# Threshold attention with hash-routed experts: expert tiles of 122 slots in place of 128, and expert 0's blocks turned elsewhere

## The chip, the cores and the metric

The kernel runs on one core of a Trainium2 chip. The metric is the device time in microseconds (us) of one execution; lower is better. The engines are TensorE (PE; its weight loads are listed apart as PEld), VectorE (DVE), ScalarE (ACT), GpSimd (POOL) and SyncE (SP), and sixteen DMA engines carry the transfers that SP and POOL issue.

## What is computed

Attention with a threshold, over 8 batches of 8 heads with 576 rows of 64, is followed by a layer of 8 experts. A token's expert is a hash of its id, with no learned gate, and each token goes to exactly one expert. All is float32.

```python
# attention: batch 8, heads 8, seq 576, head_dim 64
scores = scale * np.matmul(q, k.transpose(0, 1, 3, 2))
thresh = np.max(scores, axis=-1, keepdims=True) - tau
scores = np.where(scores >= thresh, scores, -1000000000.0)
attn = np.exp(scores - np.max(scores, axis=-1, keepdims=True))
attn = attn / (np.sum(attn, axis=-1, keepdims=True) + 1e-09)
x = np.matmul(attn, v)            # -> (B*S, H*D) = (4608, 512)
# experts: N 4608, D 512, E 8, F 1024
expert_idx = token_ids * np.int64(2654435761) % np.int64(E)
for e in range(E):
    mask = expert_idx == e
    h = np.maximum(x[mask] @ w1[e], 0.0)
    out[mask] = h @ w2[e]
```

The inputs are drawn with a fixed seed. The token ids of that seed give the eight experts 598, 596, 571, 565, 599, 533, 570 and 576 tokens.

## The kernel before

**Attention.** The 64 pairs of batch and head are taken two heads at a time: 32 "pairs" p of five steps s, so 160 steps n = 5p + s, and six more steps drain the pipeline (L508; `LAST` is 160). A step takes 128 rows of each of its two heads; step s = 0 takes the last 64 rows of both together. The order of instructions on each engine is the order in which this loop writes them (`manual_schedule`, L500), and the engines run against one another only through tiles and their buffers:

- `score` (L173): TensorE writes the scores of a head into an `sc` tile, two PSUM banks. There are two such tiles (`ps_sc`).
- `negate` (L190): DVE copies the scores, negated, to SBUF and finds the extreme; POOL works out the threshold `thr`.
- `expo` (L206) and `mask` (L215): ACT takes the exponential, and one step later DVE zeroes what lies under the threshold and sums the rows.
- `turn_w` and `put_wT` (L239, L244): two steps later TensorE turns the masked block into the `tr` tile, of which there is one (`ps_tr`), with ten small transposes that work on 64 rows each; ACT copies it to SBUF.
- `av_part` (L254), `put_oT` (L264), `turn_o` (L268): weights times v, copied by ACT, turned back by TensorE.
- `put_xt` and `put_xm` (L282, L294): ACT and DVE divide by the row sums, and SP stores x to two scratch tensors in HBM: `xa_scratch` with the first 384 columns, `xb_scratch` with the last 128, which belong to the last eight pairs.

**Routing.** `route` (L306) runs in pieces between the steps. It ranks the tokens of each expert and scatters token numbers to `slot_scratch`, where each expert owns `CAP` = 640 slots: `KT` = 5 tiles of 128. Tokens of an expert beyond `CAP` go to overflow tiles. One load (L412) brings the slots to SBUF as `gidx`.

**Expert 0, early.** From step `G0` = 130 on, each of ten steps has POOL gather the rows of one tile from `xa_scratch` by the indices in `gidx` (`fetch`, L570), for the five tiles of expert 0 and the five of expert 1. At steps 137, 142, 147, 152 and 157 `early_xT` (L452, called at L573) turns one gathered tile of expert 0, three blocks of 128 columns, in the `tr` tile, and ACT copies it into `xT_0`. `early_h` (L461) is the first GEMM of expert 0 over these three quarters of the columns: 48 matmuls, of which `fill(1)` issues one and which are placed in the draining steps, one in step 160 and two in each of the five that follow; the rest follows the loop (L578). The last quarter can be gathered from `xb_scratch` only after the last pair's stores (L577). It is turned tile by tile, in five calls of `early_xT` (L580), and `late_h` (L476) adds its share and takes the relu.

**The experts.** For each expert (L628) `gemm1` (L597) computes h with w1 as the loaded operand and the slots as the streamed one, in two halves of `CH` = 320 columns; ACT and DVE take the relu in turn. Then for each of the five tiles `turn_x` turns a tile of the next expert (four transposes and a DVE copy, `put_xT`, L591), and `gemm2` (L613) computes 128 output rows with h as the loaded operand and 512 columns of w2 streamed; ACT copies them to `o_sb` and POOL scatters them to the output by `gidx`. The weights and gathers of the expert after next are issued meanwhile. A float32 product is two matmul instructions in the profile.

**Overflow.** A loop at the end (L645) runs once for each overflow tile, with its number of turns read from `ov_i`.

Of the kernel before, what the change touches and what calls it, by code (L numbers as in the profile page):

```python
# [9 lines left out]
FP32 = mybir.dt.float32  # L10
BF16 = mybir.dt.bfloat16
FP16 = mybir.dt.float16
I32 = mybir.dt.int32
# [7 lines left out]
def kernel(  # L21
# [12 lines left out]
    nc = tc.nc  # L34

    B, H, D, S = qT.shape
    N, DIN = out.shape
    E, _, F = w1.shape
    P = 128
# [13 lines left out]

    KT = 5
    CAP = KT * P
    CH = CAP // 2
    NOV = 32
    NSLOT = E * CAP + NOV * P  # L60
    BIG = 1 << 20
    assert all((N - (m - 1) * (CAP + 1) - CAP + P - 1) // P + m - 1 <= NOV
               for m in range(1, E + 1) if m * (CAP + 1) <= N)
# [21 lines left out]
    tau_in = consts.tile([P, 1], FP32, name="tau_in")  # L85
    keep_any = consts.tile([P, 1], FP32, name="keep_any")
    drop = consts.tile([P, 1], FP32, name="drop")
    gidx = consts.tile([P, E, KT], I32, name="gidx")
    ov_i = consts.tile([P, NOV + 1], I32, name="ov_i")


# [5 lines left out]
    def gather(x_dram, dst, idx):  # L97
        nc.gpsimd.indirect_dma_start(
            out=dst, out_offset=None, in_=x_dram[:, :],
            in_offset=bass.IndirectOffsetOnAxis(ap=idx, axis=0),  # L100
            bounds_check=N - 1, oob_is_err=False)

    def fetch(e, kt, part):
        xg = xg_bufs[(e * KT + kt) % (2 * KT)]
        dram, dst = (xa_dram, xg[:, 0:XA]) if part == 0 else (xb_dram, xg[:, XA:DIN])
        gather(dram, dst, gidx[:, e, kt:kt + 1])

    def load_w1(e):
        w1_sb = w_pool.tile([P, CO, F], FP32, name="w1_sb")
# [8 lines left out]
    with tc.tile_pool(name="a_q", bufs=1) as a_q, \  # L118
# [330 lines left out]
                                op0=ALU.mult, op1=ALU.add)  # L449
        nc.vector.tensor_tensor(out=drop[:], in0=drop[:], in1=tau_in[:], op=ALU.max)  # L450

        def early_xT(kt, cos):  # L452

            n = len(cos)
            tr = ps_tr.tile([P, 2, 512], FP32, name="tr")
            turn(tr, xg_bufs[kt], [(P * c, P * c) for c in cos])
            nc.scalar.copy(xT_0[:, cos[0]:cos[0] + n, kt * P:kt * P + P]  # L457
                           .rearrange("p c (r q) -> p r c q", r=2),
                           tr[:, :, 0:64 * n].rearrange("p r (c q) -> p r c q", c=n))

        def early_h():  # L461

# [33 lines left out]
        def fill(n):  # L496
            for _ in range(n):
                next(h_pieces, None)

        with tc.manual_schedule():  # L500

            tr = ps_tr.tile([P, 2, 512], FP32, name="tr")
            for _ in range(24):
                nc.tensor.transpose(tr[:, 0, 0:P], ident[:], ident[:])
            next(pieces)
            scale_q(0)
            score(0)
            for n in range(LAST + NS + 1):  # L508
                p, s = divmod(n, NS)
                m = n - 2  # L510
                if s == 0 and p + 2 < NP:
                    load_pair(p + 2)
                if s == 0 and p + 1 < NP:
                    load_v(p + 1)
                if s == 1 and p + 1 < NP:
                    scale_q(p + 1)
                if s == 2 and p in (20, 24):
                    load_w1(p // 4 - 5)
                if s == 2 and p in (22, 26):
                    load_w2((p - 22) // 4)  # L520

                q = p - 1
                if s == 1 and 0 <= q < NP:
                    add_eps(q)
                if s == 2 and 0 <= q < NP:
                    nc.vector.reciprocal(recs[q][:], recs[q][:])
                if s == 0 and p >= 2:
                    turn_o()
                    put_xt(p - 2)
                if s in (1, 2) and 0 <= q < NP:  # L530
                    av_part(q, 0, ((0, 1, 2), (3, 4))[s - 1])
                if n < LAST and s in (1, 2):
                    negate(n)
                    expo(n, 0)
                if s == 2 and 0 <= q < NP:
                    put_oT(0)
                if n > LAST:
                    fill(1)
# [24 lines left out]
                if 0 < n <= LAST:  # L563
                    for j in range(heads(n - 1)):
                        mask(n - 1, j)
                next(pieces, None)


                g = n - G0
                if 0 <= g < 2 * KT:  # L570
                    fetch(g // KT, g % KT, 0)
                if s == 2 and 0 <= g - KT < NS * KT:
                    early_xT((g - KT) // NS, list(range(CO - 1)))  # L573
                if n == LAST:
                    fill(1)
            for g in range(2 * KT):
                fetch(g // KT, g % KT, 1)  # L577
            fill(FO * 2 * (CO - 1) + 1)  # L578
            for kt in range(KT):
                early_xT(kt, [CO - 1])  # L580
            late_h()

    with tc.tile_pool(name="m_x", bufs=1) as m_x, \
# [4 lines left out]
        xT_bufs = [xT_0, m_x.tile([P, CO, CAP], FP32, name="xT_1")]  # L588
        h_bufs = [h_0, m_x.tile([P, FO, CAP], FP32, name="h_1")]

        def put_xT(xg, xT, kt):  # L591
            tr = ps_x.tile([P, CO, P], FP32, name="xT_ps")
            for co in range(CO):
                nc.tensor.transpose(tr[:, co], xg[:, co * P:co * P + P], ident[:])  # L594
            nc.vector.tensor_copy(xT[:, :, kt * P:kt * P + P], tr[:])  # L595

        def gemm1(w1_sb, xT, h_sb, n, width):  # L597
            for fo in range(FO):
# [11 lines left out]
                    nc.vector.tensor_scalar(out=dst, in0=h_ps[:, 0:n, 0:width], scalar1=0.0,  # L610
                                            scalar2=None, op0=ALU.max)

        def gemm2(w2_sb, h_sb, kt, idx):  # L613
            o_ps = ps_o.tile([P, DIN], FP32, name="o_ps")
            for fo in range(FO):
                nc.tensor.matmul(o_ps[:], lhsT=h_sb[:, fo, kt * P:kt * P + P],  # L616
                                 rhs=w2_sb[:, fo, :], start=(fo == 0), stop=(fo == FO - 1))
            o_sb = m_o.tile([P, DIN], FP32, name="o_sb")
            nc.scalar.copy(o_sb[:], o_ps[:])  # L619
            nc.gpsimd.indirect_dma_start(  # L620
                out=out[:, :], out_offset=bass.IndirectOffsetOnAxis(ap=idx, axis=0),
                in_=o_sb[:], in_offset=None, bounds_check=N - 1, oob_is_err=False)

        def turn_x(e, kt):
            put_xT(xg_bufs[(e * KT + kt) % (2 * KT)], xT_bufs[e % 2], kt)

        with tc.manual_schedule():
            for e in range(E):  # L628
                if e > 0:
                    gemm1(w_tiles.pop((e, 1)), xT_bufs[e % 2], h_bufs[e % 2], 2, CH)  # L630
                if e + 2 < E:
                    load_w1(e + 2)
                    for g in range(2 * KT):
                        fetch(e + 2, g // 2, g % 2)
                w2_sb = w_tiles.pop((e, 2))
                for kt in range(KT):
                    if e + 1 < E:
                        turn_x(e + 1, kt)
                    gemm2(w2_sb, h_bufs[e % 2], kt, gidx[:, e, kt:kt + 1])
                if e + 2 < E:  # L640
                    load_w2(e + 2)

# [2 lines left out]
        with tc.For_i(0, n_ov, 1) as it:  # L645
            ex = nc.values_load(ov_i[0:1, bass.ds(it, 1)], engines=[mybir.EngineType.Pool],
                                min_val=0, max_val=E - 1)
            w1_sb = w_pool.tile([P, CO, F], FP32, name="w1_sb")
            w2_sb = w_pool.tile([P, FO, DIN], FP32, name="w2_sb")
            nc.gpsimd.dma_start(  # L650
                out=w1_sb[:],
                in_=w1[bass.ds(ex, 1)].rearrange("o (c p) f -> p (o c) f", p=P))
            nc.gpsimd.dma_start(
                out=w2_sb[:],
                in_=w2[bass.ds(ex, 1)].rearrange("o (c p) d -> p (o c) d", p=P))
            idx = m_o.tile([P, 1], I32, name="idx_ov")
# [3 lines left out]
            put_xT(xg_bufs[0], xT_0, 0)  # L660
            gemm1(w1_sb, xT_0, h_0, 1, P)
            gemm2(w2_sb, h_0, 0, idx[:, 0:1])


# [32 lines left out]
```

## Time and profile before

| | us |
|---|---|
| median of four runs | 1105.46 |
| lowest and highest | 1104.05, 1107.99 |
| the profiled execution, device time | 1105.22 |
| its span, first to last instruction | 1103.6 |

The span has two stages, as the rows of busy tenths in 40 slices (27.6 us each) show:

```
PE   7999999999999999999999999999999999999996
DVE  7889899999999999886230100100101001011000
ACT  5788888888888888886020000001000000000000
POOL 3656622222222226321332214013040130101001
DMA  4132223222243546310132124213242042300000
```

Each digit is the busy share of a slice in tenths. The attention fills the first 19 slices, up to some 515 us, with TensorE, DVE and ACT all busy. Then come expert 0 and the other experts, where TensorE works nearly alone.

The largest groups of TensorE work, by line:

| line | what | instructions | busy us |
|---|---|---|---|
| L616 | second GEMM, 512 columns streamed | 640 | 280.6 |
| L602 | first GEMM of experts 1 to 7, 320 columns | 896 | 242.3 |
| L187 | scores | 1152 | 215.8 |
| L234 | transposes of 64 rows | 2880 | 161.5 |
| L260 | weights times v | 1280 | 183.5 |

The first GEMM of expert 0 is apart, 96 instructions at L468 and 32 at L482. The last scatter is issued by POOL at 1094.78 us, 8.8 us before the span's end.

In the time order, a row gives the start, the duration, the engine, the line, the operation with its output and inputs, how many were merged, and in brackets how long the engine was idle before it and what released it.

### The profile page before, as it was taken

What the parts mean: (1) busy time and instruction counts of PE and PEld (TensorE: products, weight loads), DVE (VectorE), ACT (ScalarE), POOL (GpSimd) and SP (SyncE); (2) the same over time, 40 slices, a digit from 0 to 9 for tenths busy, and PEclk for the clock granted to TensorE, in tenths of its full rate; (3) what the DMA queues carried; (4) which work ended last, traced back from release to release, by engine and by line L of the source; (5) the groups of instructions that cost most, each with busy time, mean ns of one, the idle gap of its engine ahead of it and who ended that gap; (6) DMA issues with size and microseconds to landing.
All of it is one profiled execution on the core that took longest, in us unless ns stands there. A gap on an engine that the chain in (4) does not pass through costs nothing. (4 is left out here: it accounts for less than half of the span.)

```text
span 1103.6 us, 19964 instructions
## 1 busy us (share of the span) xinstructions
PE 1078.3 (98%) x7502; PEld 670.9 (61%) x7502; DVE 518.5 (47%) x1348; ACT 483.2 (44%) x800; POOL 302.1 (27%) x396
## 2 busy tenths in 40 slices
PE   7999999999999999999999999999999999999996
PEld 6666666666666666665655746557556475564652
DVE  7889899999999999886230100100101001011000
ACT  5788888888888888886020000001000000000000
POOL 3656622222222226321332214013040130101001
PEclk7999999999999999999999999999999999999999
DMA  4132223222243546310132124213242042300000
GB/s 119 48 88 77 63 81 88 87 76 61 83 127 122 153 139 204 105 31 23 33 122 100 55 103 139 85 44 106 93 141 79 36 128 93 100 1 33 10 13 31
DMA packets 78112, 91.60 MB, mean 83 GB/s; under 512 B 17977, under 2 KB 52923, under 8 KB 78016
## 3 DMA queue, kind: packets, MB, share of 16 engines
q1 hardware_dynamic: 69824, 71.42, 21.0%
q0 software_dynamic: 8192, 18.91, 5.1%
q8 instruction: 60, 0.98, 0.4%
q14 instruction: 36, 0.29, 0.1%
HBM read 72.41 MB, written 19.98 MB: 84 GB/s over the span
## 5 line engine op out<-in xcount | busy, mean ns | idle before, releaser
L616 PE MATMUL o_ps<-w_sb,h 128*128 128x512 f32 x640 | 280.6, 592 | 0.0
L602 PE MATMUL sc<-xT,w_sb 128*128 128x320 f32 x896 | 242.3, 432 | 0.0
L210 ACT ACTIVATE w<-ns,nmx 128x576 f32<-128x576 f32 x288 | 220.3, 777 | 35.3 <-DVE ns L199 34.6
L223 DVE SCALAR_TENSOR_TENSOR w<-ns,thr,w 128x576 f32<-128x576 f32 x288 | 228.1, 824 | 0.0
L199 DVE TENSOR_SCALAR_CACHE_REDUCE ns<-sc 128x576 f32<-128x576 f32 x288 | 207.5, 753 | 38.0 <-PE sc L187 32.9
L187 PE MATMUL sc<-k_sb,q 64*128 64x288 f32 (+1 forms) x1152 | 215.8, 430 | 4.4 <-DVE ns L199 3.1
L602 PEld LDWEIGHTS sc<-xT,w_sb 128*128 128x128 f32 x896 | 170.2, 190 | 73.2 <-issue 3.3
L616 PEld LDWEIGHTS o_ps<-w_sb,h 128*128 128x128 f32 x640 | 118.9, 190 | 136.0 <-issue 135.6
L234 PEld LDWEIGHTS tr<-ident,w 64*128 64x128 f32 x2880 | 122.3, 140 | 95.1 <-ACT wT_a L252 32.2
L203 POOL TENSOR_SCALAR thr<-nmx,drop 128x2 f32<-128x2 f32 (+1 forms) x160 | 100.7, 629 | 248.8 <-DVE ns L199 243.3
L234 PE MATMUL tr<-ident,w 64*128 64x64 f32 x2880 | 161.5, 234 | 7.2 <-ACT xT L457 3.3
L620 POOL DMA_INDIRECT out_dram<-o_sb,gidx x40 | 39.7, 992 | 428.0 <-ACT o_sb L619 420.2
L619 ACT COPY o_sb<-o_ps 128x512 f32<-128x512 f32 x40 | 23.4, 585 | 293.9 <-PE o_ps L616 293.9
L610 DVE TENSOR_SCALAR h<-sc 128x640 f32<-128x640 f32 x28 | 23.1, 824 | 267.2 <-PE sc L602 193.2
L187 PEld LDWEIGHTS sc<-k_sb,q 64*128 64x128 f32 (+1 forms) x1152 | 132.5, 192 | 24.0 <-DVE ns L199 6.4
L252 ACT COPY wT_a<-tr 128x640 f32<-128x640 f32 x160 | 110.2, 689 | 28.7 <-PE tr L234 28.2
L595 DVE COPY xT<-xT_ps 128x512 f32<-128x512 f32 x35 | 24.1, 689 | 181.7 <-PE xT_ps L594 181.7
L608 ACT ACTIVATE h<-sc 128x640 f32<-128x640 f32 x28 | 19.7, 703 | 191.9 <-PE sc L602 176.0
L260 PE MATMUL av<-wT_a,v 128*64 128x320 f32 x640 | 100.3, 442 | 0.0
L252 ACT COPY wT_b<-tr 128x640 f32<-128x640 f32 x128 | 87.7, 685 | 18.5 <-PE tr L234 16.8
L260 PE MATMUL av<-wT_b,v 128*64 128x256 f32 x640 | 83.2, 389 | 0.0
L260 PEld LDWEIGHTS av<-wT_a,v 128*64 128x64 f32 x640 | 40.2, 136 | 28.8 <-issue 0.4
(91 smaller groups left out, 506.7 us busy)
## 6 DMA issues: line engine op xcount, KB each, us to landing
w_sb<-in_moe_w_dram SPq DMA_DIRECT2D x16, 2048.0 KB
k_sb<-in_k_dram SPq DMA_DIRECT2D x32, 288.0 KB
q<-in_q_dram SPq DMA_DIRECT2D x32, 256.0 KB
v<-in_v_dram SPq DMA_DIRECT2D x32, 256.0 KB
xa_scratch<-xm SPq DMA_DIRECT2D x24, 256.0 KB
xb_scratch<-xm SPq DMA_DIRECT2D x8, 256.0 KB
q<-in_q_dram SPq DMA_DIRECT2D x64, 16.0 KB
v<-in_v_dram SPq DMA_DIRECT2D x32, 32.0 KB
```

Source lines behind the costliest of these rows:

```text
L187: nc.tensor.matmul(scs[n, j][:, i, 0:S2], lhsT=q_sb[rows, cols], rhs=k_sb[rows, S2 * i:S2 * i + S2], start=True, stop=True)
L199: nc.vector.tensor_scalar(out=ns[:].rearrange("p (i s) -> p i s", i=2), in0=sc[:, :, 0:S2], scalar1=-1.0, scalar2=None, op0=ALU.mult, op1= ...
L203: nc.gpsimd.tensor_scalar(out=thr[:, 0:nj], in0=nmx[:, 0:nj], scalar1=drop[:], scalar2=None, op0=ALU.add)
L210: nc.scalar.activation(w[:, 0:S], nss[n, j][:], AF.Exp, bias=stats[n][0][:, j:j + 1], scale=-1.0)
L223: nc.vector.scalar_tensor_tensor(out=w[:, 0:S], in0=nss.pop((n, j))[:], scalar=stats[n][1][:, j:j + 1], in1=w[:, 0:S], op0=ALU.is_le, op1= ...
L234: nc.tensor.transpose(dst[:, r, 64 * c:64 * c + 64], src[rows, c0:c0 + P], ident[rows, rows])
L252: nc.scalar.copy(dst, src)
L260: nc.tensor.matmul(av[64 * j:64 * j + 64, g, 0:width], lhsT=v_bufs[p % 3][:, c, 64 * j:64 * j + 64], rhs=wT[g][:, j, c, :], start=(c == 0) ...
L595: nc.vector.tensor_copy(xT[:, :, kt * P:kt * P + P], tr[:])
L602: nc.tensor.matmul(h_ps[:, i, 0:width], lhsT=w1_sb[:, co, fo * P:fo * P + P], rhs=xT[:, co, i * width:i * width + width], start=(co == 0), ...
L616: nc.tensor.matmul(o_ps[:], lhsT=h_sb[:, fo, kt * P:kt * P + P], rhs=w2_sb[:, fo, :], start=(fo == 0), stop=(fo == FO - 1))
L620: nc.gpsimd.indirect_dma_start(out=out[:, :], out_offset=bass.IndirectOffsetOnAxis(ap=idx, axis=0), in_=o_sb[:], in_offset=None, bounds_ch ...
```

## The change

A tile of slots has `TM` = 122 rows in place of 128, so an expert owns 610 slots and the two halves of the first GEMM have 305 columns each. Gathers, transposes, output rows and scatters follow. The overflow tiles keep 128 rows.

The five early turns of expert 0 in steps 137 to 157 go. In their place the same blocks are turned in step 160 in `sc` tiles, in three groups: tiles 0 and 1, tiles 2 and 3, and tile 4, each with two ACT copies (rows 0 to 63 and rows 64 to 121). The first group stands ahead of `turn_o` and `put_xt`, the second behind them, the third behind the first `put_wT`. Step 160 now has two fills in place of one. The last quarter's columns are turned in one group in the `tr` tile with two copies, and six of the 48 fills follow it in place of none.

```diff
-    KT = 5
-    CAP = KT * P
+    KT, TM = 5, 122
+    CAP = KT * TM
     CH = CAP // 2
     NOV = 32
-    NSLOT = E * CAP + NOV * P
+    NSLOT = -(-(E * CAP + NOV * P) // P) * P
...
-    gidx = consts.tile([P, E, KT], I32, name="gidx")
+    gidx = consts.tile([TM, E, KT], I32, name="gidx")
...
-        gather(dram, dst, gidx[:, e, kt:kt + 1])
+        gather(dram, dst[0:TM], gidx[:, e, kt:kt + 1])
...
-        def early_xT(kt, cos):
-
-            n = len(cos)
-            tr = ps_tr.tile([P, 2, 512], FP32, name="tr")
-            turn(tr, xg_bufs[kt], [(P * c, P * c) for c in cos])
-            nc.scalar.copy(xT_0[:, cos[0]:cos[0] + n, kt * P:kt * P + P]
-                           .rearrange("p c (r q) -> p r c q", r=2),
-                           tr[:, :, 0:64 * n].rearrange("p r (c q) -> p r c q", c=n))
+        def early_xT(tr, k0, k1, c0, c1):
+
+            blocks = [(kt, co) for kt in range(k0, k1) for co in range(c0, c1)]
+            dst = xT_0[:, c0:c1, k0 * TM:k1 * TM].rearrange("p c (k q) -> p k c q", k=k1 - k0)
+            for i, (kt, co) in enumerate(blocks):
+                for r, r1 in ((0, 64), (64, TM)):
+                    nc.tensor.transpose(tr[:, r // 64, 64 * i:64 * i + r1 - r],
+                                        xg_bufs[kt][r:r1, P * co:P * co + P],
+                                        ident[r:r1, r:r1])
+            for r, r1 in ((0, 64), (64, TM)):
+                src = tr[:, r // 64, 0:64 * len(blocks)].rearrange(
+                    "p (k c q) -> p k c q", k=k1 - k0, c=c1 - c0)
+                nc.scalar.copy(dst[:, :, :, r:r1], src[:, :, :, 0:r1 - r])
...
+                if n == LAST:
+                    tr = ps_sc.tile([P, 2, 512], FP32, name="sc")
+                    early_xT(tr, 0, 2, 0, CO - 1)
                 if s == 0 and p >= 2:
                     turn_o()
                     put_xt(p - 2)
+                if n == LAST:
+                    tr = ps_sc.tile([P, 2, 512], FP32, name="sc")
+                    early_xT(tr, 2, 4, 0, CO - 1)
...
                 if turned:
                     tr = turn_w(m, 0)
                     put_wT(m, 0, tr)
-                if n > LAST:
+                if n == LAST:
+                    tr = ps_sc.tile([P, 2, 512], FP32, name="sc")
+                    early_xT(tr, 4, 5, 0, CO - 1)
+                if n >= LAST:
                     fill(1)
...
-                if s == 2 and 0 <= g - KT < NS * KT:
-                    early_xT((g - KT) // NS, list(range(CO - 1)))
                 if n == LAST:
                     fill(1)
             for g in range(2 * KT):
                 fetch(g // KT, g % KT, 1)
-            fill(FO * 2 * (CO - 1) + 1)
-            for kt in range(KT):
-                early_xT(kt, [CO - 1])
+            fill(FO * 2 * (CO - 1) - 18)
+            tr = ps_tr.tile([P, 2, 512], FP32, name="tr")
+            early_xT(tr, 0, KT, CO - 1, CO)
+            fill(18)
             late_h()
...
-        def put_xT(xg, xT, kt):
+        def put_xT(xg, xT, kt, rows):
             tr = ps_x.tile([P, CO, P], FP32, name="xT_ps")
             for co in range(CO):
-                nc.tensor.transpose(tr[:, co], xg[:, co * P:co * P + P], ident[:])
-            nc.vector.tensor_copy(xT[:, :, kt * P:kt * P + P], tr[:])
+                nc.tensor.transpose(tr[:, co, 0:rows], xg[0:rows, co * P:co * P + P],
+                                    ident[0:rows, 0:rows])
+            nc.vector.tensor_copy(xT[:, :, kt * rows:kt * rows + rows], tr[:, :, 0:rows])
...
-        def gemm2(w2_sb, h_sb, kt, idx):
+        def gemm2(w2_sb, h_sb, kt, idx, rows):
             o_ps = ps_o.tile([P, DIN], FP32, name="o_ps")
             for fo in range(FO):
-                nc.tensor.matmul(o_ps[:], lhsT=h_sb[:, fo, kt * P:kt * P + P],
+                nc.tensor.matmul(o_ps[0:rows], lhsT=h_sb[:, fo, kt * rows:kt * rows + rows],
                                  rhs=w2_sb[:, fo, :], start=(fo == 0), stop=(fo == FO - 1))
             o_sb = m_o.tile([P, DIN], FP32, name="o_sb")
-            nc.scalar.copy(o_sb[:], o_ps[:])
+            nc.scalar.copy(o_sb[0:rows], o_ps[0:rows])
             nc.gpsimd.indirect_dma_start(
                 out=out[:, :], out_offset=bass.IndirectOffsetOnAxis(ap=idx, axis=0),
-                in_=o_sb[:], in_offset=None, bounds_check=N - 1, oob_is_err=False)
+                in_=o_sb[0:rows], in_offset=None, bounds_check=N - 1, oob_is_err=False)
```

The calls of `turn_x`, `gemm2` and `put_xT` pass 122 for the experts' tiles and 128 for the overflow tiles.

More of the change, by code (lines that the diff above doesn't have):

```diff
@@ L611, in gemm1 @@
                                             scalar2=None, op0=ALU.max)
-        def gemm2(w2_sb, h_sb, kt, idx):
+        def gemm2(w2_sb, h_sb, kt, idx, rows):
             o_ps = ps_o.tile([P, DIN], FP32, name="o_ps")
             for fo in range(FO):
-                nc.tensor.matmul(o_ps[:], lhsT=h_sb[:, fo, kt * P:kt * P + P],
+                nc.tensor.matmul(o_ps[0:rows], lhsT=h_sb[:, fo, kt * rows:kt * rows + rows],
                                  rhs=w2_sb[:, fo, :], start=(fo == 0), stop=(fo == FO - 1))
             o_sb = m_o.tile([P, DIN], FP32, name="o_sb")
-            nc.scalar.copy(o_sb[:], o_ps[:])
+            nc.scalar.copy(o_sb[0:rows], o_ps[0:rows])
             nc.gpsimd.indirect_dma_start(
                 out=out[:, :], out_offset=bass.IndirectOffsetOnAxis(ap=idx, axis=0),
-                in_=o_sb[:], in_offset=None, bounds_check=N - 1, oob_is_err=False)
+                in_=o_sb[0:rows], in_offset=None, bounds_check=N - 1, oob_is_err=False)
         def turn_x(e, kt):
-            put_xT(xg_bufs[(e * KT + kt) % (2 * KT)], xT_bufs[e % 2], kt)
+            put_xT(xg_bufs[(e * KT + kt) % (2 * KT)], xT_bufs[e % 2], kt, TM)
         with tc.manual_schedule():
@@ L638 @@
                         turn_x(e + 1, kt)
-                    gemm2(w2_sb, h_bufs[e % 2], kt, gidx[:, e, kt:kt + 1])
+                    gemm2(w2_sb, h_bufs[e % 2], kt, gidx[:, e, kt:kt + 1], TM)
                 if e + 2 < E:
@@ L659 @@
             gather(xb_dram, xg_bufs[0][:, XA:DIN], idx[:, 0:1])
-            put_xT(xg_bufs[0], xT_0, 0)
+            put_xT(xg_bufs[0], xT_0, 0, P)
             gemm1(w1_sb, xT_0, h_0, 1, P)
-            gemm2(w2_sb, h_0, 0, idx[:, 0:1])
+            gemm2(w2_sb, h_0, 0, idx[:, 0:1], P)
 _LAYOUTS = {
```

## The prediction

> **What bounds the kernel now.** I first read the engine shares on the page, then the busy time by stage, then the order of instructions at the places that the change touches.
>
> ```profile
> PE 1078.3 (98%) x7502; PEld 670.9 (61%) x7502; DVE 518.5 (47%) x1348; ACT 483.2 (44%) x800; POOL 302.1 (27%) x396
> ```
>
> 98% is an average over two stages. From 563 us, where only expert matmuls run, the stretches answer (stretch, then each engine's busy time, granted clock, DMA share, GB/s):
>
> ```profile
> 600.00:1000.00 400.00, 400.00 (x1299) 236.48 (x1298) 37.88 (x51) 32.09 (x50) 77.06 (x77) 1.00 0.26 89
> 1000.00:1093.30 93.30, 93.30 (x276) 50.92 (x274) 5.37 (x7) 7.49 (x12) 7.86 (x8) 1.00 0.05 21
> ```
>
> TensorE is never idle there, at the full clock, and DVE, ACT and the DMA engines are mostly empty: every ns taken off a matmul comes off the span. What a column costs is read from starts in TensorE's time order:
>
> ```profile
> 570.21 7.03 PE L616 MATMUL o_ps<-w_sb,h 128*128 128x512 f32 x16
> 577.08 0.60 PE L594 MATMUL xT_ps<-ident,xg 128*128 128x128 f32 x4
> 577.51 7.03 PE L616 MATMUL o_ps<-w_sb,h 128*128 128x512 f32 x16
> ...
> 599.00 34.62 PE L602 MATMUL sc<-xT,w_sb 128*128 128x320 f32 x128
> 633.45 0.60 PE L594 MATMUL xT_ps<-ident,xg 128*128 128x128 f32 x4
> ```
>
> Sixteen 512-column matmuls take 577.08 - 570.21 = 6.87 us, 429.4 ns each; 128 of 320 columns take 633.45 - 599.00 = 34.45 us, 269.1 ns each. (The mean in the groups, 432 ns, is one matmul's latency, not its spacing.) The difference gives 160.3 / 192 = 0.835 ns a column and 1.9 ns fixed.
>
> The attention stage is a ring instead: TensorE turns a block into the one tr tile, ACT copies it out, TensorE may turn the next. Its step for the early blocks of expert 0:
>
> ```profile
> 506.36 0.38 PE L234 MATMUL tr<-ident,xg 64*128 64x64 f32 x6
> ...
> 506.86 0.47 ACT L457 COPY xT<-tr 128x384 f32<-128x384 f32 x1
> ...
> 507.38 0.53 PE L234 MATMUL tr<-ident,w 64*128 64x64 f32 x10 [0.64 <-ACT xT L457]
> ```
>
> The next score block could have been turned where the x block was; it starts 507.38 - 506.36 = 1.02 us later, behind the copy. One instruction per head pair shows that this reaches the pair's period:
>
> ```profile
> 343.81 0.20 DVE L526 RECIPROCAL rec<-rec 128x9 f32<-128x9 f32 x1
> 359.13 0.20 DVE L526 RECIPROCAL rec<-rec 128x9 f32<-128x9 f32 x1
> ...
> 470.20 0.20 DVE L526 RECIPROCAL rec<-rec 128x9 f32<-128x9 f32 x1
> 486.56 0.20 DVE L526 RECIPROCAL rec<-rec 128x9 f32<-128x9 f32 x1
> ```
>
> 15.32 us without an early turn, 16.36 with one.
>
> **The change, part by part.**
>
> *Narrower first GEMM.* 320 columns become 305. L602 runs 896 matmul instructions (each fp32 product is two), L468 96, L482 32: 1024 x 15 x 0.835 ns = 12.8 us, of which 11.2 lie in the gap-free stage. Ends: 0 if width didn't count, 12.9 by proportion (269.1 x 15/320 = 12.6 ns each). I take 12.8, since two widths lie on one line. The weight load of 190 ns stays beside a matmul of 256.6.
>
> *Second GEMM, turns, copies.* L616 still streams 512 columns; 122 slots only narrow its weights, whose load hides beside 429 ns: nothing. The four turns of a block take 577.51 - 577.08 = 0.43 us; streaming 122 for 128 columns would save 0.02 us on each of 35, 0.7 in all, but the operand loaded is still 128 columns wide. I take 0. The Trainium skill, "TensorE: Matmul & The Clock Gate", section LDWEIGHTS, makes a weight load cost its columns, not its rows; by it these turns save nothing, by the streamed width 0.7 us. The narrower copies on DVE and ACT (0.82, 0.70 and 0.69 us in steps of over 2 us) were hidden already: nothing.
>
> *Five early turns leave the attention loop.* The interval after 437.39 us, and the four after it, hold one each. The first four are 16.44, 16.37, 16.36 and 16.31 against 15.32, and the first still holds two gathers; the fifth isn't comparable, for the scores run out, so it gets the 1.02 of its ring step. Sum 1.12 + 1.05 + 1.04 + 0.99 + 1.02 = 5.2 us. The interval before (16.82) has gathers on POOL and no turn; its excess stays. Ends: 4.1 (the four at 1.02) to 5.7.
>
> *They come back at step 160*, as 30 transposes and six ACT copies, with no DMA of their own. Space for them:
>
> ```profile
> 513.49 0.69 ACT L252 COPY wT_a<-tr 128x640 f32<-128x640 f32 x1
> ...
> 514.23 0.53 PE L234 MATMUL tr<-ident,w 64*128 64x64 f32 x10 [0.73 <-ACT wT_a L252]
> ...
> 515.60 0.53 PE L234 MATMUL tr<-ident,w 64*128 64x64 f32 x10 [0.84 <-ACT wT_b L252]
> ```
>
> Ten transposes take about 0.45 us to the next start, so 30 take 1.35, and TensorE idles 0.73 + 0.84 = 1.57 there. The score banks are free: the last negation of scores ends at 512.3, before this step. ACT is tighter. Its copies cost 0.83 ns a column and 0.16 fixed (0.478 at 384, 0.266 at 128): 2 x (0.48 + 0.45) + 0.32 + 0.30 = 2.5 us. Behind the first two wait put_xt's two scalings; behind those put_xm on DVE, the masks of step 159, POOL's add_eps and SP's stores of pair 30, none with a reader inside the next 2 us. Behind the next two waits wT_b, and so the single tr tile. The new fill waits for the second bank's copies. Laying these in order, starts overlapping by 0.1 us as in the trace, the first av_part of pair 31 moves from 516.80 to 517.9. One extra fill (two matmuls, 0.5 us) is done by then and missing later, so the net is +0.6; ends 0 (all in the 1.57) and +2.5 (all copies on the path). I take +0.8.
>
> *Last column block in one go.*
>
> ```profile
> 550.69 0.28 PE L234 MATMUL tr<-ident,xg 64*128 64x64 f32 x2
> ...
> 551.32 0.27 PE L234 MATMUL tr<-ident,xg 64*128 64x64 f32 x2 [0.36 <-ACT xT L457]
> ...
> 553.43 6.94 PE L482 MATMUL sc<-xT,w_sb 128*128 128x320 f32 x24
> ```
>
> Five turn-and-copy rounds keep the matmuls away for 553.43 - 550.69 = 2.74 us. Ten transposes take some 0.6, and the two copies (0.43 + 0.40) hide beside six fills, 12 x 257 ns = 3.1 us: -2.1. The turns now come six fills sooner, so their gathers matter: the fifth is issued by 540.67. The 32 fills after turn_o at 529.04 end at 529.5 + 64 x 0.257 = 545.9 on the same clock, 5 us after the issue; a gather later than that would be a new wait. Ends -2.7 and +1.
>
> *Sum.* -12.8 - 5.2 + 0.8 - 2.1 = -19.3 us against the profiled execution's 1105.22 (span 1103.6 and 1.6 around it; 0.24 under the median): 1085.9. On the median it is 1086.2; I say **1086**.
>
> **What the trace doesn't show** is an indirect transfer of other than 128 rows. The last scatter moves 0.24 MB in some 0.7 us (about three slices of 0.25 us at 254 to 410 GB/s), on 16 engines, and the program ends behind it. All rows on one engine would take 16 x 0.7 = 11 us: ends 0 and +10.5. I take 0, since 122 rows are as many descriptors less six. Gathers of later experts have some 80 us of cover (issued from 552, turned from 633) and the index load 275 (issued at 142, read from 417): nothing. Here a rule speaks against the change: the skill's "DMA: Bandwidth & Descriptors", section on why a DMA increments its semaphore by 16, has the engine count as the largest divisor up to 16 of the slowest dimension, which is 16 for 128 and 2 for 122. By it the last scatter would take 8 x 0.7 = 5.6 us, and the sum would be 1091; it also tells of an exception for some direct copies that spread unevenly, by which it stays 1086.
>
> **Rivals.** *A slow tail*: 122-row scatters use few engines. For it: 122 isn't a multiple of 16, and nothing covers the last one. Against: earlier ones have 6 us between them. At the middle of 0 and +10.5, 1091; at the far end, with the gathers of the last column block also late by some 4, 1100. *The width gains nothing*: the second half starts 1220 bytes into a row, where every operand so far starts on a multiple of 64 (1152, 1280). Then 1086 + 12.8 = 1099. Against: the straight line over two widths. *Slower*: the same odd starts uncover the weight loads of L602, L468 and L482. Each is 190 ns and hidden now; a quarter exposed costs 1024 x 48 ns = 49 us, 1135. It decides from (12.8 + 6.5) / 1024 = 19 ns exposed per matmul. Against: four turns run in 0.43 us with loads of 141 ns each, so loads overlap under much shorter matmuls. *It doesn't do what it says*: an expert with over 610 tokens would run the overflow loop. The seeded ids give 533 to 599 per expert; excluded.
>
> **How the numbers follow.** Forecast 0.65 (own range 1083.5 to 1089: widths 0.3, loop 1.1, step 160 0.8 down and 1.7 up, turns 0.7 down), slow tail 0.18, no width gain 0.07, slower 0.07, the rest, 0.03, near no change. What this kernel's measurement can tell from no change is about 0.3%, 3.3 us: faster 0.90, same 0.03, slower 0.07. 1082.5 to 1094 holds the forecast and most of the slow tail.
>
> **What would show it.** Width: 128 matmuls of L602 in 32.85 us from first start to the next turn; slower means a moving-operand cost. Loop: pair periods of 15.3 at 453 to 502 us. Step 160: av_part of pair 31 about 5.8 us after the last turn of step 157 starts (4.7 now). Last block: under 1 us between the early matmuls before and after the ten transposes; a DMA as releaser there means late gathers. Tail: the last POOL scatter to the span's end, now 8.8 us; 13 or more means few engines. A time above 1094 means the first or the last of these failed.

## The result, and the profile after

The changed kernel takes **1107.0 us** (median of 52 runs, 1101.79 to 1112.7); the kernel before took 1104.48 us in the 78 runs beside them (1101.32 to 1111.1). The ratio of the means is 1.0019, 95% interval 1.0011 to 1.0027. The prediction was 1086, 1082.5 to 1094, so nothing of the forecast gain is to be seen. The profiled execution of the changed kernel took 1106.97 us, with a span of 1105.4.

The page after: the shares of the engines, and the queue that carries the indirect transfers (packets, MB, share of 16 engines' span), its second row from the kernel before:

```profile
PE 1066.0 (96%) x7502; PEld 664.6 (60%) x7502; DVE 514.8 (47%) x1348; ACT 481.6 (44%) x798; POOL 386.5 (35%) x396
...
q0 software_dynamic: 41472, 19.32, 7.6%
...
q0 software_dynamic: 8192, 18.91, 5.1%
```

TensorE is busy 12.3 us less. That is not yet the narrower GEMM by itself, for the moved turns and some matmuls at a lower clock are in it too. But POOL is busy 84.4 us longer with the same 396 instructions, and the queue needs 41472 packets where before it needed 8192 for about as many bytes (18.91 MB). The groups of POOL's indirect transfers, the gathers from `xb_scratch` and the scatters, each after and then before:

```profile
L98 POOL DMA_INDIRECT xg<-xb_scratch,gidx x40 | 69.1, 1727 | 33.1 <-issue 32.2
...
L98 POOL DMA_INDIRECT xg<-xb_scratch,gidx x40 | 40.1, 1002 | 32.7 <-DMA xb_scratch<-xm 17.0 <-issue 9.8 <-PE tr L234 4.4
...
L634 POOL DMA_INDIRECT out_dram<-o_sb,gidx x40 | 66.9, 1673 | 357.7 <-issue 212.8
...
L620 POOL DMA_INDIRECT out_dram<-o_sb,gidx x40 | 39.7, 992 | 428.0 <-ACT o_sb L619 420.2
```

One scatter occupies POOL for 1673 ns, where it took 992, and a gather for 1727, where it took 1002. Where that reaches the time is seen at the end, in POOL's and ACT's time order of the changed kernel, with the last copy and scatter of the kernel before below it:

```profile
1051.22 0.58 ACT L633 COPY o_sb<-o_ps 122x512 f32<-122x512 f32 x1 [10.34 <-PE o_ps L630]
1052.10 1.66 POOL L634 DMA_INDIRECT out_dram<-o_sb,gidx  x1 [25.94 <-ACT o_sb L633]
1058.08 0.58 ACT L633 COPY o_sb<-o_ps 122x512 f32<-122x512 f32 x1 [6.28 <-PE o_ps L630]
1062.06 1.67 POOL L634 DMA_INDIRECT out_dram<-o_sb,gidx  x1 [8.29 <-DMA out_dram<-o_sb,gidx]
...
1078.68 0.58 ACT L633 COPY o_sb<-o_ps 122x512 f32<-122x512 f32 x1 [6.28 <-PE o_ps L630]
1082.71 1.67 POOL L634 DMA_INDIRECT out_dram<-o_sb,gidx  x1 [8.73 <-DMA out_dram<-o_sb,gidx]
1093.33 1.66 POOL L634 DMA_INDIRECT out_dram<-o_sb,gidx  x1 [8.95 <-issue]
...
1093.92 0.58 ACT L619 COPY o_sb<-o_ps 128x512 f32<-128x512 f32 x1 [6.28 <-PE o_ps L616]
1094.78 0.98 POOL L620 DMA_INDIRECT out_dram<-o_sb,gidx  x1 [5.88 <-ACT o_sb L619]
```

ACT's copies of the last expert come every 6.87 us, as before. The scatters, in the rows shown and the one left out between them, start every 10 to 10.6 us, and what releases them is not the copy but the landing of the scatter before (they all write the same output tensor). The last row names only "issue", but it too starts some 1 us after the landing before it, at 1092.11. So each of the five is later than its copy by more, and the last starts 14.1 us after its copy ended at 1079.26; before, 0.28 us. The chain of waits gives the landings themselves (start, duration, what the chain passes through), here the shortest and the longest of four, and one of the kernel before:

```profile
1052.10 9.05 DMA out_dram<-o_sb,gidx
...
1072.31 9.48 DMA out_dram<-o_sb,gidx
...
1081.05 2.71 DMA out_dram<-o_sb,gidx
```

From the start on POOL to the landing it takes 9.1 to 9.5 us, where it took 2.7. How the two move is told by the stretch around one scatter, in forty slices: the mean busy share of the 16 DMA engines in tenths, and the rate. First the kernel before, slices of 0.2 us from 1080 us:

```profile
DMA  0000000000000998000000000000000000000000
GB/s 0 0 0 0 0 0 0 0 0 0 0 0 0 471 369 318 21 0 0 0 0 0 0 0 0 0 0 0 0 0 0 0 0 0 0 0 0 0 0 0
```

Then the last scatter of the changed kernel, slices of 0.3 us from 1093 us:

```profile
DMA  0000000003420121010111111011110000000000
GB/s 0 0 0 0 0 0 0 0 2 5 31 28 0 14 27 14 0 55 41 41 55 55 55 55 55 41 55 55 55 41 20 0 0 0 0 0 0 0 0 0
DMA packets 512, 0.24 MB, mean 20 GB/s; under 512 B 454, under 2 KB 454, under 8 KB 512
```

The same 0.24 MB goes out with eight or nine tenths of the sixteen engines' time busy before, and mostly with one tenth after (as much as about two engines), at up to 55 GB/s instead of some 320 to 470. It also goes in 512 packets, where the scatter of before took 80 (22 of them under 512 bytes, by the same view). The 58 packets of 2 KB and more are as many in both; 454 small ones stand beside them in place of 22.

The second place is the last column block of expert 0, TensorE's time order after:

```profile
540.23 0.40 PE L458 MATMUL tr<-ident,xg 64*128 64x64 f32 x6
541.84 0.27 PE L458 MATMUL tr<-ident,xg 64*128 64x64 f32 x2 [1.22 <-DMA xg<-xb_scratch,gidx]
543.99 0.36 PE L458 MATMUL tr<-ident,xg 64*128 64x64 f32 x2 [1.87 <-DMA xg<-xb_scratch,gidx]
544.28 6.11 PE L473 MATMUL sc<-xT,w_sb 128*128 128x305 f32 x12
550.22 8.88 PE L487 MATMUL sc<-xT,w_sb 128*128 128x305 f32 x32
```

Three of the five gathers are there in time. The fourth and fifth hold the turns up for 1.22 + 1.87 = 3.1 us, and the twelve matmuls behind them take 550.22 - 544.28 = 5.94 us where twelve by 256.8 ns make 3.1. The stretch from 540 us says why (busy time and count of each engine, then granted clock, DMA share, GB/s):

```profile
540.00:550.00 10.00, 6.91 (x24) 4.47 (x23) 0.80 (x1) 0.73 (x2) 8.47 (x6) 0.66 0.16 33
```

The granted clock is 0.66 on the mean there; the matmuls ran at about half rate behind the pause.

### The profile page after: what moved, and what is told of

Its sections match the earlier page's. It is cut to its first block, busy times and chain, and to the rows that moved or that the text cites. A ratio compares the mean times of both kernels' runs of the same rounds, so it can differ in the third digit from the quotient of the medians.

```text
span 1105.4 us, 19958 instructions
## 1 busy us (share of the span) xinstructions
PE 1066.0 (96%) x7502; PEld 664.6 (60%) x7502; DVE 514.8 (47%) x1348; ACT 481.6 (44%) x798; POOL 386.5 (35%) x396
## 3 DMA queue, kind: packets, MB, share of 16 engines
q1 hardware_dynamic: 69762, 71.42, 21.3%
q0 software_dynamic: 41472, 19.32, 7.6%
## 4 chain that ended last, share of the span: by engine, by line
PE 88%; DMA 5%; issue 3%; ACT 2%; DVE 1%; POOL 0%; SPq 0%; POOLq 0%; ACTq 0%; DVEq 0%
PE o_ps L630 22%; PE sc L616 19%; PE sc L187 16%; PE av L260 15%; PE tr L234 11%; DMA out_dram<-o_sb,gidx 4%; PE xT_ps L607 1%; PE sc L473 1%; PE av L234 1%; PE sc L487 1%; ACT wT_a L252 1%; DMA xg<-xb_scratch,gidx 0%; ACT w L210 0%; ACT wT_b L252 0%; DVE ns L199 0%
## 5 line engine op out<-in xcount | busy, mean ns | idle before, releaser
L630 PE MATMUL o_ps<-w_sb,h 128*122 128x512 f32 x640 | 280.6, 592 | 0.0
L616 PE MATMUL sc<-xT,w_sb 128*128 128x305 f32 x896 | 231.2, 419 | 0.0
L187 PE MATMUL sc<-k_sb,q 64*128 64x288 f32 (+1 forms) x1152 | 213.1, 427 | 2.2 <-DVE ns L199 1.6
L630 PEld LDWEIGHTS o_ps<-w_sb,h 128*122 128x122 f32 x640 | 115.6, 185 | 138.9 <-issue 138.5
L634 POOL DMA_INDIRECT out_dram<-o_sb,gidx x40 | 66.9, 1673 | 357.7 <-issue 212.8
L633 ACT COPY o_sb<-o_ps 122x512 f32<-122x512 f32 x40 | 23.4, 585 | 293.5 <-PE o_ps L630 293.5
L187 PEld LDWEIGHTS sc<-k_sb,q 64*128 64x128 f32 (+1 forms) x1152 | 130.7, 191 | 20.9 <-DVE ns L199 3.9
L624 DVE TENSOR_SCALAR h<-sc 128x610 f32<-128x610 f32 x28 | 22.2, 793 | 256.9 <-PE sc L616 256.9
L609 DVE COPY xT<-xT_ps 128x488 f32<-128x488 f32 x35 | 23.2, 664 | 183.4 <-PE xT_ps L607 183.4
L622 ACT ACTIVATE h<-sc 128x610 f32<-128x610 f32 x28 | 19.0, 679 | 182.6 <-PE sc L616 182.6
L98 POOL DMA_INDIRECT xg<-xb_scratch,gidx x40 | 69.1, 1727 | 33.1 <-issue 32.2
```

What stands on the lines that cost most here:

```text
L98: nc.gpsimd.indirect_dma_start(out=dst, out_offset=None, in_=x_dram[:, :], in_offset=bass.IndirectOffsetOnAxis(ap=idx, axis=0), bounds_che ...
L187: nc.tensor.matmul(scs[n, j][:, i, 0:S2], lhsT=q_sb[rows, cols], rhs=k_sb[rows, S2 * i:S2 * i + S2], start=True, stop=True)
L616: nc.tensor.matmul(h_ps[:, i, 0:width], lhsT=w1_sb[:, co, fo * P:fo * P + P], rhs=xT[:, co, i * width:i * width + width], start=(co == 0), ...
L630: nc.tensor.matmul(o_ps[0:rows], lhsT=h_sb[:, fo, kt * rows:kt * rows + rows], rhs=w2_sb[:, fo, :], start=(fo == 0), stop=(fo == FO - 1))
L634: nc.gpsimd.indirect_dma_start(out=out[:, :], out_offset=bass.IndirectOffsetOnAxis(ap=idx, axis=0), in_=o_sb[0:rows], in_offset=None, boun ...
```

## The experiments

Four readings were to be told apart: that indirect transfers of 122 rows are slow (in the gathers, in the scatters or both); that their chain on POOL, and not each one's own length, costs the time; that the size itself, 122, is bad, for its divisors; and that the other parts of the change (the widths, the moved turns) brought less than was forecast. Every edit is to the changed kernel. To compare profiles whose routing stage took unequally long (see the end), the span is cut at two instructions: the **path** goes from one head pair's reciprocal, at 401 to 408 us, to the end of the last copy to `o_sb`, and the **tail** from there to the span's end. Each has one profile. A ratio is to runs of the kernel before on the same occasion, with medians of 1102.3 to 1105.19; the kernels after the first two rows have 4 to 10 runs each.

| kernel | median us | ratio to before | path | tail |
|---|---|---|---|---|
| before | 1104.48 | | 689.2 | 9.1 |
| the change, 122 rows | 1107.0 | 1.0019 [1.0011, 1.0027] | 676.6 | 26.1 |
| 128 rows moved | 1081.74 | 0.9818 [0.9793, 0.9842] | 668.7 | 9.0 |
| the same again | 1083.12 | 0.9802 [0.9762, 0.9843] | 668.7 | 9.1 |
| tiles of 120 | 1082.35 | 0.9808 [0.9779, 0.9837] | 664.3 | 9.5 |
| tiles of 124 | 1093.52 | 0.9915 [0.9892, 0.9938] | 674.6 | 13.9 |
| turns alone, tiles of 128 | 1096.3 | 0.9943 [0.9924, 0.9962] | 683.6 | 9.0 |
| scatters of 128, gathers of 122 | 1086.94 | 0.9849 [0.9818, 0.9879] | 671.9 | 7.2 |
| gathers of 128, scatters of 122 | 1115.48 | 1.011 [1.0077, 1.0142] | 682.5 | 27.0 |
| the same again | 1101.34 | 0.9969 [0.995, 0.9988] | 670.4 | 26.9 |
| two targets for the scatters | 1092.24 | 0.9886 [0.9852, 0.992] | 673.4 | 12.8 |
| tiles of 120, 128 rows moved | 1091.22 | 0.988 [0.9856, 0.9905] | 676.9 | 9.3 |
| the same again | 1078.05 | 0.9766 [0.9727, 0.9805] | 664.2 | 9.1 |
| the same, turns four fills later | 1078.26 | 0.9775 [0.9737, 0.9813] | 664.1 | 9.0 |

**128 rows moved.** The computation keeps its 122 slots; only the transfers are padded to 128 rows, with indices past the end for the six.

```diff
-    gidx = consts.tile([TM, E, KT], I32, name="gidx")
+    gidx = consts.tile([P, E, KT], I32, name="gidx")
...
-        gather(dram, dst[0:TM], gidx[:, e, kt:kt + 1])
+        gather(dram, dst, gidx[:, e, kt:kt + 1])
...
-            nc.sync.dma_start(out=gidx[:], in_=slot_dram[0:E * CAP].rearrange(
+            nc.sync.dma_start(out=gidx[0:TM], in_=slot_dram[0:E * CAP].rearrange(
...
+        nc.gpsimd.memset(gidx[:], BIG)
...
+        o_bufs = [m_x.tile([P, DIN], FP32, name=f"o_{i}") for i in range(4)]
+        for o_sb in o_bufs:
+            nc.vector.memset(o_sb[:], 0.0)
...
-            o_sb = m_o.tile([P, DIN], FP32, name="o_sb")
+            o_sb = o_bufs[o_count[0] % 4]
...
-                in_=o_sb[0:rows], in_offset=None, ...
+                in_=o_sb[:], in_offset=None, ...
```

> Tiles of 122 slots as in the changed kernel, but every gather and scatter of expert tiles moves 128 rows; the last six have an index beyond the bound and are skipped. Theory A (the 122-row indirect transfers run on few DMA engines, and each scatter waits on POOL for the one before it to land): scatters take POOL 0.98 us and land some 2.7 us after their start, the wait of 3.1 us for the last column block's gathers goes, and the last scatter starts 0.3 us behind its copy: 1107.0 less 17.0 (five chained scatters, 53.3 us from the first one's start to the end of the span against 36.3) less 3.3, about 1087. Theory C (the transfers are slow because of something else in the change, such as the odd starts in the tiles): still 1104 to 1108.

1081.74 us. Everything but the transfers is the change as it was (the four `o_sb` buffers are zeroed once, so that the six rows hold something), and the whole loss is gone. That is 5 us less than expected: the path is 7.9 us shorter than in the change, not only by the wait of 3.1, as the stretches at a low clock went too (see below). POOL's scatters are back at 0.98 us each, are released by the copy, and land 2.7 us after their start. TensorE's time order in the last column block:

```profile
537.60 0.52 PE L459 MATMUL tr<-ident,xg 64*128 64x64 f32 x10
538.06 3.35 PE L474 MATMUL sc<-xT,w_sb 128*128 128x305 f32 x12
541.24 8.88 PE L488 MATMUL sc<-xT,w_sb 128*128 128x305 f32 x32
```

The ten turns run in one go and the twelve fills behind them take 541.24 - 538.06 = 3.18 us, with no wait. Measured again beside later kernels it gave the same path to 0.1 us.

> The kernel with 122 slots and 128-row transfers once more, beside the next two on one chip: 0.981 to 0.983 of the kernel before, with no stall in the last column block. A ratio near 0.99 would mean that the stall seen with 120 slots comes by chance to any of these kernels.

**Tiles of 120 and of 124.** One number each, `KT, TM = 5, 120` and `KT, TM = 5, 124`; nothing is padded.

> Tiles of 120 slots, transfers of 120 rows. Theory A with the engine count as the largest divisor of the row count up to 16: 15 engines, scatters land in 3 to 3.5 us, no chain. TensorE saves 5 more columns on 1024 matmuls, 4.3 us at 0.835 ns: about 1083. Theory B (any row count but 128 loses the packets of 4 KB and the engines): scatters of 9.5 us and more stay chained, five take some 53 us from a first start 4 us earlier: about 1103. The Trainium skill, DMA: Bandwidth & Descriptors, section on why a DMA increments its semaphore by 16, states the divisor rule.

> Tiles of 124 slots, transfers of 124 rows. Theory A with the divisor rule: 4 engines. The changed kernel's scatter takes 9.5 us, of which some 2 are there with 16 engines too; half of the other 7.5 makes 5.8 us, under the 6.9 us of a block of the second GEMM, so nothing is chained and only the last one is about 3 us late. TensorE has 5 columns more on 1024 matmuls than with 122, 4.3 us: about 1087 + 4.3 + 3, 1094. Theory B: the chain stays, about 1108 to 1110.

With 120 rows a scatter lands after 3.2 us, occupies POOL for 0.99 us, and the queue needs 8192 packets again: 1082.35 us, though only two rows are taken from each tile. With 124 a scatter lands after 6.4 to 7.1 us and occupies POOL for 1.32, and the queue needs 22912 packets: 1093.52 us. The rate around one scatter with 124 rows, in slices of 0.3 us from 1081 us:

```profile
DMA  0000000004282001222222100000000000000000
GB/s 0 0 0 0 0 0 0 0 0 45 42 41 14 0 0 41 68 68 82 109 109 82 48 34 7 0 0 0 0 0 0 0 0 0 0 0 0 0 0 0
```

Two tenths of the engines for most of it, and up to twice the rate of 122. Its scatters start 7.7 to 8.0 us apart, so they chain too, but only by about 1 us each, hence a tail of 13.9. (The 1094 expected had been worked out with landings of 5.8 us and no chain, so it is in part luck that the number fits.) So it isn't that fewer than 128 rows are slow: 122 is slower than both its neighbours.

**The turns alone.** `KT, TM = 5, 128`: the moved turns and the last block in one go, at the old tile size.

> The changed kernel with tiles of 128 slots: only the turns are moved. By the prediction's terms -5.2 (loop), +0.8 (step 160) and -2.1 (last block) against the kernel before: 6.5 us less, about 1098, with pair periods of 15.3 us and no wait for a gather. If the moved turns gave their gain back at step 160: 1103 to 1105.

Its path is 5.6 us shorter than before, its median 6.0 us under the kernel before beside it (1102.3); the prediction's terms for this part, -5.2, +0.8 and -2.1, make -6.5.

**Scatters or gathers padded alone.** From the padded kernel, one side is put back to 122 rows:

```diff
-        gather(dram, dst, gidx[:, e, kt:kt + 1])
+        gather(dram, dst[0:TM], gidx[0:TM, e, kt:kt + 1])
```

and, in the other kernel, the scatters as in the change, with `gidx[0:TM, e, kt:kt + 1]` as their index.

> Tiles of 122 slots, scatters of 128 rows, gathers of 122. Theory A: the tail of the run with 128-row transfers (last scatter 0.3 us behind its copy), but TensorE again waits some 3 us for the last column block's gathers and then has some 3 us at half clock: about 6 us above that run, 15 us under the kernel before. Rival (the gathers carry the loss): no more than 5 us under the kernel before.

> Tiles of 122 slots, gathers of 128 rows, scatters of 122. Theory A: no wait for the gathers, so the last expert starts some 6 us sooner than in the changed kernel, but its five scatters stay chained, some 53 us from the first one's start to the end of the span: 3 to 5 us under the kernel before. Rival (the gathers carry the loss): 20 us under the kernel before.

With slow gathers alone the turns wait 2.9 us for the fourth and fifth; in the profiled run the clock stayed at full speed and the path is 3.2 us longer than with all padded (671.9 against 668.7). This profile is of the fastest of its four runs, 1081.93 us; the others took 1086.84 to 1089.54. (That its tail is 1.8 us shorter than that of all padded was not followed up.) With slow scatters alone the tail is 27.0 us, as in the change. But this kernel's path held something more, a stall of 7.0 us in TensorE's last column block, while DVE stood idle for 10.1 with its scores done, and a granted clock of 0.76 from 546 to 560 us. None of its waits there names a transfer. The kernel was measured again on another chip:

> The kernel with gathers of 128 rows and scatters of 122 once more. Its first measurement stood above the changed kernel, with a stall of 7 us in the last column block of the same kind as the one that was gone when the kernel with 120 slots was measured again. If that stall was chance: five chained scatters, 53 to 54 us from the first one's start to the end of the span, and TensorE some 6 us ahead of the changed kernel: 0.995 to 0.998 of the kernel before. If the stall belongs to scatters of 122 rows: again about 1.01.

1101.34 us, without the stall. The last two of its scatters start at 1077.24 and 1087.53 us, each released by the landing before it, and the tail is 26.9. The chained scatters alone thus leave 3.85 us of the gain (1101.34 against 1105.19), where all padded leaves 20.56 (1081.74 against 1102.3): they cost some 17 us. The gathers alone cost 4.2 (16.34 of the gain is left, 1086.94 against 1103.28). The two make 20.9 of the 23.1 us between the change and all padded (20.56 and the 2.5 lost); the rest is not assigned.

**Two targets.** Tiles 1 and 3 of each expert are scattered to a second tensor, so that a scatter waits for the one before the last. The output then lacks these rows; the kernel serves only for its time. The scatters are as slow as in the change.

```diff
+    alt_dram = nc.dram_tensor("alt_scratch", (N, DIN), FP32, kind="Internal").ap()
...
-                out=out[:, :], out_offset=...
+                out=dst[:, :], out_offset=...
...
-                    gemm2(w2_sb, h_bufs[e % 2], kt, gidx[:, e, kt:kt + 1], TM)
+                    gemm2(w2_sb, h_bufs[e % 2], kt, gidx[:, e, kt:kt + 1], TM,
+                          (out, alt_dram)[kt % 2])
```

> The changed kernel, 122 rows throughout, but tiles 1 and 3 of each expert are scattered to a scratch tensor of the same shape, so these rows are left out of the output. A scatter then waits only for the last but one. If the wait of each scatter for the one before turns 9.5 us into the tail: the last scatter starts right behind its copy and ends 12 us later, about 14 us under the changed kernel, some 11 to 13 under the kernel before. Rival (two engines are all that the scatters have, with or without the wait): they land no faster, 0 to 3 us under the changed kernel.

POOL's time order at the end:

```profile
1065.40 1.67 POOL L635 DMA_INDIRECT out_dram<-o_sb,gidx  x1 [5.19 <-ACT o_sb L634]
1072.27 1.67 POOL L635 DMA_INDIRECT alt_scratch<-o_sb,gidx  x1 [5.21 <-ACT o_sb L634]
1079.47 1.67 POOL L635 DMA_INDIRECT out_dram<-o_sb,gidx  x1 [5.53 <-ACTq L661]
```

The scatters now start 6.9 to 7.2 us apart, each right behind its copy, though a landing still takes 9.2 to 9.6 us. The tail falls from 26.1 to 12.8: the last scatter's own length is all that is left. The waiting, and not the rate by itself, makes most of the tail.

**120 and 128 together.** Tiles of 120 with the transfers padded to 128 rows, then the same measured again, then with two fills in place of six behind the turns (`fill(FO * 2 * (CO - 1) - 14)` and `fill(14)`).

> Tiles of 120 slots and transfers of 128 rows, the two together. Theory A: 5 columns less on 1024 matmuls than with 122 slots and 128 rows, 4.3 us at 0.835 ns: 24 to 25 us under the kernel before, a ratio of about 0.977 to 0.978. Rival (something else ends the program by then): no better than with 122 slots, 0.981 to 0.982.

> The kernel with 120 slots and 128-row transfers once more. It stood some 13 us over its sum, and its profile has a stall of 8.6 us, where TensorE's signal for its last fill reached DVE 10 us late. If the stall belongs to this program: again about 0.988 of the kernel before. If it was chance or the chip: 0.977 to 0.978.

> As the run with 120 slots and 128-row transfers, but the last column block is turned four fills later, so that two fills follow it in place of six. The two copies, 0.8 us, still fit beside the two fills' 1.0 us, so the sum is the same. If the stall depends on where the turns meet the stream of gathers: 0.977 to 0.979. If it doesn't: 0.988.

The first measurement missed: 1091.22 us, with all six runs between 1089.45 and 1093.86. TensorE's time order of its profiled run, in the last column block:

```profile
544.14 1.28 PE L488 MATMUL sc<-xT,w_sb 128*128 128x300 f32 x4 [0.69 <-ACT xT L465]
554.05 2.37 PE L488 MATMUL sc<-xT,w_sb 128*128 128x300 f32 x4 [8.64 <-DVE h L478]
```

TensorE waits 8.6 us for a copy by DVE of the last fill's scores. DVE starts that copy at 553.22 after 12.63 us of idleness, though the matmuls it reads had ended by 543.5. The same kernel measured again on the same chip gave 1078.05 us and no such wait, and the version with the turns later gave 1078.26: one and the same within their intervals. So the stall belongs to neither the kernel nor the chip as such; its cause is open. The version with tiles of 120 moved as 128 rows beats both kernels: 0.9766, 0.9727 to 0.9805, and 0.988 with the stall.

## Why the prediction was wrong

The step that failed is the one under "What the trace doesn't show": an indirect transfer of 122 rows was taken at 0 on top of one of 128, "since 122 rows are as many descriptors less six". The two bounds, 0 and +10.5 us, were made for one late scatter at the end. The rival "slow tail" had the mechanism, but set aside its larger half with "earlier ones have 6 us between them". A landing of 9.5 us doesn't fit into 6.87 us, and each scatter waits for the one before. The working, with what was measured:

- *The tail.* The excess over before is 26.1 - 9.1 = 17.0 us. 13.8 of it (14.1 - 0.3) is the last scatter's waiting, summed up over five in a chain, and 3.3 its own length, 12.1 us to the span's end in place of 8.8. Against the value taken, 0, that is the loss of nearly the whole gain. The sign named for it, the last scatter to the span's end at 13 us or more, looked in the wrong place: that stretch grew only to 12.1.
- *The gathers.* "A gather later than that would be a new wait" is what came. The margin of 5 us was counted from an issue at 540.67; but POOL now issues one every 2.03 us (1.72 and 0.30 between) in place of 1.30, and the fifth, at 538.68, lands after 5.26. In the profiled run the wait took 3.1 us and the half clock behind it 5.94 - 3.18 = 2.8.
- *Step 160* was right: in the padded kernel the first av_part of pair 31 starts 6.06 us after the last turn of step 157 instead of 4.66, with one more fill (0.5 us) done, net +0.9 against +0.8. In the change's own profile the granted clock was 0.88 from 510 to 520 us and twelve matmuls of av_part took 3.02 us in place of 1.84.
- *The width* was right: 128 matmuls take 1044.11 - 1011.24 = 32.87 us, 256.8 ns each, 12.3 ns less than before; times 1024 that is 12.6 us (12.8). A matmul that starts 1220 bytes into a row costs nothing more, so both rivals built on that fall.
- *The four turns* were taken at nothing and saved a little: 0.42 us for four where it was 0.43, about 0.5 us over 35 times.
- *The loop* was right: from the reciprocal at 405.31 to that at 517.35 the kernel before takes 112.04 us, the changed one, from 402.69 to 509.32, 106.63: -5.4 (-5.2).
- *The last block in one go* was right once the gathers are in time: -2.3 in the padded kernel (-2.1).

So the sum was sound for what it counted: -19.3 was forecast, and the two measurements of the padded kernel, which differs from the change in its transfers alone, stand 20.6 and 21.3 us under the kernel before beside them. On the path the profile of the padded kernel is 20.5 us shorter than before; -12.6 - 0.5 - 5.4 + 0.9 - 2.3 make 19.9, and 0.6 us is not assigned. The changed kernel's path is 7.9 us longer than the padded one's: 6.4 from the first turn of the last block to the late matmuls (540.23 to 550.22, against 537.60 to 541.24), 1.5 before it, where the clock was low at step 160. 12.6 us gained on the path and 17.0 lost in the tail leave +4.4; the profiled run's earlier start, 402.69 against 405.31, takes 2.6 off, and the spans differ by +1.8.

On the rule that the prediction weighed and didn't follow: the Trainium skill, "DMA: Bandwidth & Descriptors", section "Why a DMA increments its semaphore by 16 and not by 1", has the number of engines as the largest divisor up to 16 of the slowest dimension. For 128, 120, 124 and 122 rows that is 16, 15, 4 and 2. The runs agree: 2.7, 3.2, 6.4 to 7.1 and 9.1 to 9.5 us from start to landing, with up to nine tenths of the engines' time busy for the first two and mostly two and one tenths for the others. The profile shows that share and not which engines ran, so the count itself is inferred. The exception that the page tells of, for some direct copies that spread unevenly, doesn't show in these indirect transfers. The estimate made from it, 5.6 us of moving for a scatter, fell short: the last one's bytes move for some 6.9 us (23 slices of 0.3). Besides, each scatter has 432 more packets under 512 bytes, and POOL's own work is longer (1.66 us against 0.98). How much each of these adds was not tried apart. And the estimate was made for the last scatter alone, without the chain.

## What to carry to other kernels

When an edit changes the number of rows in an indirect transfer, that transfer is a new operation: its price is measured at the new size, and at a neighbour or two, before anything is counted as saved; the padding of the transfers back to 128 rows, with indices past the end, kept the narrower computation and cost nothing measurable (with tiles of 120 the path is 664.2 us padded and 664.3 not). Where several transfers write one tensor, the landing time must be compared with the interval at which they come: up to it a slow one costs its own length once, beyond it every one adds the difference, and the last one carries the sum. A rival whose "against" is an interval needs that comparison with its own far bound, here 11 us against 6.9.

## What the runs showed of the hardware

- The time of an indirect transfer is not monotonic in its rows: 120 rows 3.2 us, 122 rows 9.5, 124 rows 6.4 to 7.1, 128 rows 2.7 from start to landing; in packets over the whole kernel 8192, 41472, 22912 and 8192.
- The granted clock fell behind short pauses in some runs and not in others. Behind the wait for gathers it was 0.66 in the changed kernel's profile and 1.00 with the same wait in two experiments (the scatters padded alone, and the two targets). What decides it is open.
- Twice a signal from TensorE seems to have come late: to DVE by 9.8 and 7.2 us, and just before to ACT, whose copies of the last block started 3.7 and 2.5 us after the first turn in place of 0.6. By the times it was so in every run of one measurement, and in none of the same kernel's next (1091.22 against 1078.05 us, 1115.48 against 1101.34).
- The times of the kernel before lie between 1101.32 and 1111.1 us. Among the profiles such differences arise early, while the routing runs: the ninth pair's reciprocal lies between 155.9 and 162.8 us, and from there to the one at 401 to 408 all of them take 245.3 to 245.6.
